# Other places in SBUF for g and its halves, and another tile for the first chunk's lower attended values

## The chip, the cores and the metric

The kernel runs on one core of a Trainium2 chip. What counts is the device time in microseconds of one execution, the median over several runs. Beside it there is one execution taken by the hardware profiler: its page gives totals for each engine, the chain of waits that ended last, and groups of instructions; its trace can be asked for single instructions and for stretches of time. TensorE is written PE there (PEld is its loading of stationary tiles, which overlaps the matmuls), VectorE is DVE, ScalarE is ACT, GpSimd is POOL, SyncE is SP, which issues all the transfers here. L488 means line 488 of the kernel before.

## What is computed

An attention layer is followed by a feed-forward layer. Cut to what matters:

```python
# q, k, v: (4, 8, 768, 64) = batch, heads, positions, head dim
k_sum = k.reshape(B, H, nb, 32, D).max(axis=3)      # 24 block maxima
v_sum = v.reshape(B, H, nb, 32, D).mean(axis=3)     # 24 block means
scores_l = scale * q @ k.T, kept where |i - j| < 16, else -1e9
scores_s = scale * q @ k_sum.T + log(32)
a = softmax(concat([scores_l, scores_s]))
x = a @ concat([v, v_sum])                          # -> (3072, 512)

h = x @ w_in                                        # (3072, 2048)
r = maximum(h, 0)
g = s * (r * r) + b
out = g @ w_out                                     # (3072, 512)
```

All is float32. The attention part is small; the two products of the feed-forward layer are most of the work.

## The kernel before

**Chunks and blocks.** The 3,072 positions are cut into 12 chunks (c = 0 to 11) of T = 256. In a chunk the attention is done for four pairs of heads, and its result, the attended values, stands as 128 partitions by 4 blocks of 256 columns. The feed-forward layer goes through 16 blocks of 128 hidden units (f = 0 to 15). For each f the hidden product (function `hidden`, line 444) makes a PSUM tile `ph` of 128 x 256 out of the attended values and the weights w_in of the block; `activate` makes r, the square of its positive part; `scaled` makes g = s r + b on GpSimd (line 466); and the projection (`project`, line 488) adds the block's part to two PSUM tiles `po` of 128 x 512, one for each half of the chunk's positions. `evict` copies them out and stores them.

**Products in three terms.** From chunk 1 on, and for the second half of the blocks in chunk 0 (the list THREE), each float32 operand is split into an upper part rounded to the matmul's shorter type (fp32r) and a lower part that holds the rest: weights into wh and wl, attended values into xh and xl, g into gh and gl. A product is then three matmul terms: lower times upper, upper times lower, upper times upper. In the hidden product the stationary operand is a block of weights and the moving operand is xh or xl, 256 columns wide. In the projection it is the other way round: gl or gh is stationary, and wh or wl, 512 columns wide, moves. The splits are made by `attended` and `attended_low` (line 410) for x and by `split_rows` (lines 471 and 473) for g. The first half of the blocks in chunk 0 is computed in plain float32, with an undivided g0 that uses the buffers of gh.

**The first chunk's halves.** Chunk 0's attended values stand in float32. `first_upper` and `first_lower` (line 419) make their halves x0h and x0l, which the hidden products of chunk 0's blocks 8 to 15 read.

**Where tiles lie.** Tiles come from pools; a pool gives each tag a fixed number of buffers, and a new tile of the tag takes a buffer once all readers of the tile before it are done. The ones that matter:

| pool | tags | what for |
|---|---|---|
| slots | slot, 16 buffers of 4 KB | raw weights as they are loaded, the pairs of wh, at the start also kq, vn, pT0, x0h, x0l |
| wring | ring, 33 of 2 KB | whole weights wf, lower weights wl |
| stage | stage, 4 of 3 KB | raw k and v, results on their way out |
| p2 | xh 2, xl 2 of 4 KB; r 2, g 2, gh 8, gl 7 of 1 KB; pT, pr and small ones | the attended values, r, g and its halves |
| p3 | qk 4, vw 4 | the attention's operands |

In the compiled program the pools lie one behind the other in SBUF, p3 behind p2 at the end.

**What sets the order.** Each engine runs its instructions in the order in which the program writes them. For the first part, up to somewhat over a fifth of the span, that is a list written out by hand (FIRST_ORDER): `Xh` and `Xl` are the two halves of chunk 0, `y1.0` the lower attended values of chunk 1's first pair, `y2.0` those of chunk 2, `iN` and `oN` the loads of weights, `H`, `J`, `G`, `g` and `P` the hidden product, activation, scaling, split and projection. After that a regular plan takes over: four hidden products, then the projection of four blocks whose g has been made meanwhile, with the attention of the next chunk set between them. In the trace a full visit is thus 48 hidden matmuls (4 blocks x 3 terms x 4 slices), then 24 projection matmuls (4 blocks x 2 halves x 3 terms). SP issues the transfers in order too, and holds the next ones back while one waits for its buffer.

Of the kernel before, what the change touches and what calls it, by code (L numbers as in the profile page):

```python
# [11 lines left out]
F32 = mybir.dt.float32  # L12
F32R = mybir.dt.float32r
# [6 lines left out]
P = 128  # L20
# [9 lines left out]
T = NSUB * SUB  # L30
# [4 lines left out]
NKC = DM // P  # L35
# [9 lines left out]
def windowed_attention_then_relu2_ffn(ctx, tc, qk, vwin, kt, vt, kq, vrow, wp, out):  # L45
# [5 lines left out]
    slots = ctx.enter_context(tc.tile_pool(name="slots", bufs=NF))  # L51
    wring = ctx.enter_context(tc.tile_pool(name="wring", bufs=2 * NF + 1))
    stage = ctx.enter_context(tc.tile_pool(name="stage", bufs=4))
    p2 = ctx.enter_context(tc.tile_pool(name="p2", bufs=2))
    p3 = ctx.enter_context(tc.tile_pool(name="p3", bufs=3))
    ps_po = ctx.enter_context(tc.tile_pool(name="ps_po", bufs=2, space=bass.MemoryType.PSUM))
    ps_h = ctx.enter_context(tc.tile_pool(name="ps_h", bufs=2, space=bass.MemoryType.PSUM))
# [1 line left out]
    ps_t = ctx.enter_context(tc.tile_pool(name="ps_t", bufs=1, space=bass.MemoryType.PSUM))  # L59
    ps_v = ctx.enter_context(tc.tile_pool(name="ps_v", bufs=1, space=bass.MemoryType.PSUM))  # L60

    ident = const.tile([P, P], F32, name="ident")
    sb_col = const.tile([P, 2], F32, name="sb_col")
    s_col, b_col = sb_col[:, 0:1], sb_col[:, 1:2]
# [177 lines left out]
    qk_t, vw_t, ps_of, pr_of, mn_of, sm_of, pt_of, pT_of, o_of, xt, xl = ({} for _ in range(11))  # L242
# [153 lines left out]
    def attended_part(c, p):  # L396
        kcs = slice(p, p + (1 if c < 2 else 2))
        return kcs, o_of[c, p][:, : (kcs.stop - p) * T].rearrange("p (k t) -> p k t", t=T)
# [6 lines left out]

    def attended_low(c, p):
        if p == 0:
            xl[c] = p2.tile([P, NKC, T], F32R, name="xl")
        kcs, o = attended_part(c, p)
        nc.vector.tensor_tensor(xl[c][:, kcs], o, xt[c][:, kcs].bitcast(F32), ALU.subtract)  # L410

# [3 lines left out]
        copy(other, xt["first"], xt[0])  # L415

    def first_lower():
        xl["first"] = slots.tile([P, NKC, T], F32R, name="x0l", tag="slot")
        nc.vector.tensor_tensor(xl["first"], xt[0], xt["first"].bitcast(F32), ALU.subtract)


# [37 lines left out]

    def scaled(c, f, other=False):  # L460
        if c == 0 and f not in THREE:
            g = p2.tile([P, T], F32, name="g0", tag="gh", bufs=8)
        else:
            g = p2.tile([P, T], F32, name="g")
        gg[c, f] = (g,)
        (nc.vector if other else nc.gpsimd).tensor_scalar(g, r_of.pop((c, f)), s_col, b_col, ALU.mult, ALU.add)  # L466

    def split_rows(c, f):
        (g,) = gg[c, f]
        gh = p2.tile([P, T], F32R, name="gh", tag="gh", bufs=8)  # L470
        nc.vector.tensor_copy(gh, g)  # L471
        gl = p2.tile([P, T], F32R, name="gl", bufs=7)
        nc.vector.tensor_tensor(gl, g, gh.bitcast(F32), ALU.subtract)  # L473
        gg[c, f] = gh, gl

# [60 lines left out]
    def of(fn, s):  # L536
# [5 lines left out]
        "W": keep_warm, "K": k_max, "k": fill_k, "Z": scores_of_maxima, "S": scores, "M": masked, "E": exps,  # L542
        "N": normalize, "T": transposes, "C": turned, "V": values, "U": values_of_means, "R": mean_of_rows,
        "L": load_k, "F": mean_done, "t": fill_v, "X": attended, "y": attended_low, "Xh": first_upper, "Xl": first_lower,
        "Ai": of(scale_weights, "in"), "Ao": of(scale_weights, "out"), "Bi": of(convert_weights, "in"),
        "Bo": of(convert_weights, "out"), "D": lambda f: convert_weights(("in", f), ("out", f)),
        "Y": hidden_part, "H": hidden, "J": activate, "G": scaled, "g": split_rows, "P": project, "O": evict,
        "hi": of(upper_weights, "in"), "ho": of(upper_weights, "out"), "li": of(lower_weights, "in"),
        "lo": of(lower_weights, "out"),
# [22 lines left out]
    for c in range(2, NC):  # L572
        bi, ci = place(c)
        for p in range(NPAIR):
            base, v_at = NF * (c - 1) - 1, (9, 10, 4, 5)[p]
            tr = 8 + 4 * (p // 2)
            lags = (1, 1, 1, 2, (12, 13, 11, 11)[p], tr, tr, 16, 17)
            m, e0, e1, n, fv, tr, tu, va, xa = (base + lag for lag in lags)
            if ci == 0:
                then(base - 12 + p, LOAD, load_k, bi, p)  # L580
                then(base - 7 + p, ATT, k_max, bi, p)
                if p < 2:
                    for third in range(3):
                        then(base + v_at - 5 + third, LOAD, load_v, bi, p, third)
                        then(base + v_at - 1 + third // 2, ATT, v_sum, bi, p, third)
                    then(base + v_at + 1, ATT, v_mean, bi, p)
            then(base - 6, LOAD, load_unit, c, p)
            then(base + v_at, LOAD, load_values, c, p)
            then(base - 2, ATT, fill_k, c, p)
            for j in range(2):  # L590
                then(base, VISIT, scores, c, p, j)
                then(m, NEXT if p < 2 else ATT, masked, c, p, j)
                then((e0, e1)[j], NEXT if p < 2 else ATT, exps, c, p, j)
            then(n, ATT, normalize, c, p)
            then(fv, ATT, fill_v, c, p)
            then(tr, PE_ATT, transposes, c, p)
            then(tu, CHAIN, turned, c, p)
            then(va, VISIT, values, c, p)
            if p % 2 == 0:
                then(xa, ATT, attended, c, p)  # L600
                then(xa, ATT, attended_low, c, p)
# [4 lines left out]
    for i in range(NF, NC * NF):  # L606
        c, j = divmod(i, NF)
        f = steps(c)[j]

        then(i - i % 4, HID, hidden, c, f)  # L610
        for stage_of in (activate, scaled, split_rows):
            then(i, CHAIN, stage_of, c, f)
        then((i + 4) | 3, PROJ, project, c, f)
        if j == NF - 1:
            for t in range(T // P):
                then((i + 4) | 3, EVICT, evict, c, t)
# [60 lines left out]
```

## Time and profile before

| | |
|---|---|
| median of 3 runs | 631.02 us (630.45 to 631.4) |
| the profiled execution | 630.93 us, its span 629.2 us |
| granted TensorE clock | 1.00 |
| busy: PE, PEld | 616.5 us (98%), 550.7 us (88%) |
| busy: DVE, ACT, POOL | 328.3 us (52%), 308.7 us (49%), 187.7 us (30%) |
| transfers | 66.45 MB, most of them in the first fifth |

How to read it: the records of matmuls are pipelined and overlap, so a record's length is not its cost. Its cost is the distance from its start to the start of the next one. In the chain of waits such records are merged, so "5.50 PE po L488 x24" says that 24 projection matmuls in a row took 5.50 us of the chain. A row of a cut into stretches gives the stretch, its length, and then the busy time and the number of instructions of each engine in it.

### The profile page before, as it was taken

To read this page: it belongs to the slowest core of one execution; us is meant where nothing else is said; L and a number is where in the kernel's file an instruction comes from. 1 tells how busy PE (TensorE), PEld (TensorE's weight loads), DVE (VectorE), ACT (ScalarE), POOL (GpSimd) and SP (SyncE) were. 2 spreads that over 40 slices of the span, in tenths; PEclk is the share of its full clock that TensorE was granted. 3 is DMA by queue.
4 is the path that set the end of the run, shared out by engine and by line. 5 is a ranking of instruction groups with operands and counts; after the bars stand their busy time and mean duration, and the time that the engine had idled before them with its cause. 6 is when DMAs were issued, how large, how long until landed. Compare 5 with 4: busy or idle time off the path is not lost.

```text
span 629.2 us, 14328 instructions
## 1 busy us (share of the span) xinstructions
PE 616.5 (98%) x5330; PEld 550.7 (88%) x5330; DVE 328.3 (52%) x1092; ACT 308.7 (49%) x939; POOL 187.7 (30%) x351
## 2 busy tenths in 40 slices
PE   6999999999999999999999999999999999999997
PEld 5757878989989998999899999998998999899896
DVE  6999899865354246345454335336435324523311
ACT  4999975453463364265245426436345336323321
POOL 3126442211511422322242331341151151232211
PEclk9999999999999999999999999999999999999999
DMA  8999503006205015203502211600710500200000
GB/s 333 413 416 416 222 26 126 17 2 190 79 18 181 1 44 200 74 19 102 165 20 87 94 44 38 236 19 1 218 62 7 181 0 19 85 2 1 34 1 33
DMA packets 26997, 66.45 MB, mean 106 GB/s; under 512 B 3824, under 2 KB 3824, under 8 KB 26928
## 3 DMA queue, kind: packets, MB, share of 16 engines
q1 hardware_dynamic: 26928, 65.54, 29.3%
q8 instruction: 42, 0.69, 0.5%
q14 instruction: 27, 0.22, 0.1%
HBM read 59.09 MB, written 6.29 MB: 104 GB/s over the span
## 4 chain that ended last, share of the span: by engine, by line
PE 87%; DVE 4%; ACT 2%; issue 1%; POOL 1%; DVEq 0%; POOLq 0%; ACTq 0%
PE po L488 40%; PE ph L444 38%; PE pav L394 3%; PE pt L358 3%; PE ps L308 3%; DVE wf_out L141 1%; POOL g L466 1%; DVE wl_in L155 1%; DVE wf_in L141 0%; DVE wf_in L139 0%; ACT r L458 0%; DVE wf_out L139 0%; ACT wraw L125 0%; ACT wraw L126 0%; ACT r L452 0%
## 5 line engine op out<-in xcount | busy, mean ns | idle before, releaser
L466 POOL TENSOR_SCALAR g<-r,sb_col 128x256 f32<-128x256 f32 x189 | 127.1, 673 | 379.2 <-ACT r L458 256.0
L471 DVE CAST gh<-g 128x256 fp32r<-128x256 f32 x184 | 54.9, 298 | 244.0 <-POOL g L466 244.0
L452 ACT ACTIVATE r<-ph 128x256 f32<-128x256 f32 x179 | 67.6, 378 | 206.1 <-PE ph L444 187.0
L488 PE MATMUL po<-wh,gl 128*128 128x512 f32 x368 | 146.3, 397 | 0.0
L488 PE MATMUL po<-wh,gh 128*128 128x512 f32 x368 | 145.0, 394 | 0.0
L488 PE MATMUL po<-wl_out,gh 128*128 128x512 f32 x368 | 144.2, 392 | 0.0
L444 PE MATMUL ph<-xh,wl_in 128*128 128x256 f32 x704 | 109.9, 278 | 0.1
L444 PE MATMUL ph<-xl,wh 128*128 128x256 f32 x704 | 108.8, 276 | 0.0
L444 PE MATMUL ph<-xh,wh 128*128 128x256 f32 x704 | 108.7, 276 | 0.0
L473 DVE TENSOR_TENSOR gl<-g,gh 128x256 fp32r<-128x256 f32 x184 | 85.8, 466 | 33.6 <-PE po L488 16.4
L444 PEld LDWEIGHTS ph<-xh,wl_in 128*128 128x128 f32 x704 | 96.8, 188 | 4.8 <-issue 0.5
L444 PEld LDWEIGHTS ph<-xl,wh 128*128 128x128 f32 x704 | 93.6, 188 | 0.0
L444 PEld LDWEIGHTS ph<-xh,wh 128*128 128x128 f32 x704 | 93.0, 188 | 0.0
L339 ACT ACTIVATE pr<-pr,mn 128x120 f32<-128x120 f32 x176 | 67.0, 382 | 38.6 <-DVE mn L326 38.4
L458 ACT ACTIVATE r<-r 128x256 f32<-128x256 f32 x184 | 77.0, 418 | 15.2 <-DVE r L454 9.7
L488 PEld LDWEIGHTS po<-wh,gl 128*128 128x128 f32 x368 | 69.1, 188 | 14.8 <-issue 1.4
L488 PEld LDWEIGHTS po<-wh,gh 128*128 128x128 f32 x368 | 69.2, 188 | 14.3
L488 PEld LDWEIGHTS po<-wl_out,gh 128*128 128x128 f32 x368 | 69.2, 188 | 13.8
L270 POOL COPY vw<-vsum 24x256 f32<-24x256 f32 x88 | 41.7, 503 | 20.9 <-DMA vsum<-vmean 9.5
L230 ACT COPY o<-po 128x512 f32<-128x512 f32 x24 | 14.0, 589 | 42.3 <-PE po L488 41.3
L339 ACT ACTIVATION_READ_ACCUMULATOR pr<-pr,mn 128x1 f32 x176 | 33.0, 187 | 0.0
L349 DVE TENSOR_TENSOR pr<-pr,rs 128x480 f32<-128x480 f32 x48 | 32.0, 666 | 1.7
(90 smaller groups left out, 565.4 us busy)
## 6 DMA issues: line engine op xcount, KB each, us to landing
wraw<-in_wp_dram SPq DMA_DIRECT2D x32, 512.0 KB
qk<-in_qk_dram SPq DMA_DIRECT2D x44, 369.0 KB
vw<-in_vwin_dram SPq DMA_DIRECT2D x48, 256.0 KB
out_dram<-o SPq DMA_DIRECT2D x24, 256.0 KB
kraw<-in_kt_dram SPq DMA_DIRECT2D x12, 384.0 KB
vraw<-in_vt_dram SPq DMA_DIRECT2D x12, 252.0 KB
kq<-in_kq_dram SPq DMA_DIRECT2D x4, 512.0 KB
vraw<-in_vt_dram SPq DMA_DIRECT2D x6, 264.0 KB
```

The source lines that it names most:

```text
L270: nc.gpsimd.tensor_copy(vw_t[c, p][WIN:KR, e], vsum[bi][WIN : WIN + NB, 2 * p + e, :].unsqueeze(1).to_broadcast([NB, NSUB, D]),)
L308: nc.tensor.matmul(o, qi, kw[r, i, :], start=True, stop=True)
L339: nc.scalar.activation(pr, pr, AF.Exp, bias=mn_of[c, p][:, n : n + 1], scale=-1.0, accum_out=sm_of[c, p][:, n : n + 1])
L349: nc.vector.tensor_tensor(pr, pr, rs.unsqueeze(2).to_broadcast([P, 4, KR]), ALU.mult)
L358: nc.tensor.transpose(pt_of[c, p][:KR, n * P : (n + 1) * P], pr[:, n, :], ident)
L444: nc.tensor.matmul(ph, w[:, kc * P : (kc + 1) * P], x[:, kc], start=(n == 0), stop=(n == len(terms) - 1))
L452: nc.scalar.activation(r, ph, AF.Relu)
L458: nc.scalar.activation(r, r, AF.Square)
L466: (nc.vector if other else nc.gpsimd).tensor_scalar(g, r_of.pop((c, f)), s_col, b_col, ALU.mult, ALU.add)
L471: nc.vector.tensor_copy(gh, g)
L473: nc.vector.tensor_tensor(gl, g, gh.bitcast(F32), ALU.subtract)
L488: nc.tensor.matmul(po[t], a[:, t * P : (t + 1) * P], w, start=(f == steps(c)[0] and n == 0), stop=(f == steps(c)[-1] and n == len(terms) - 1),
```

## The change

Three things are done. A new pool `pg` is opened between p2 and p3; its first tile, `gap`, is 128 bytes a partition and is never used. The tiles g, g0, gh and gl come out of `pg`, with the same numbers of buffers as before. And x0l, the lower half of chunk 0's attended values, is a tile of p2's tag xl, whose two buffers the later chunks' xl use too, and no longer a tile of the slots.

```diff
+    pg = ctx.enter_context(tc.tile_pool(name="pg", bufs=1))
     p3 = ctx.enter_context(tc.tile_pool(name="p3", bufs=3))
...
+    pg.tile([P, 32], F32, name="gap")
...
     def attended_low(c, p):
         if p == 0:
-            xl[c] = p2.tile([P, NKC, T], F32R, name="xl")
+            xl[c] = p2.tile([P, NKC, T], F32R, name="xl", tag="xl")
...
     def first_lower():
-        xl["first"] = slots.tile([P, NKC, T], F32R, name="x0l", tag="slot")
+        xl["first"] = p2.tile([P, NKC, T], F32R, name="x0l", tag="xl")
...
     def scaled(c, f, other=False):
         if c == 0 and f not in THREE:
-            g = p2.tile([P, T], F32, name="g0", tag="gh", bufs=8)
-        else:
-            g = p2.tile([P, T], F32, name="g")
+            g = pg.tile([P, T], F32, name="g0", tag="gh", bufs=8)
+        else:
+            g = pg.tile([P, T], F32, name="g", bufs=2)
...
     def split_rows(c, f):
         (g,) = gg[c, f]
-        gh = p2.tile([P, T], F32R, name="gh", tag="gh", bufs=8)
+        gh = pg.tile([P, T], F32R, name="gh", tag="gh", bufs=8)
         nc.vector.tensor_copy(gh, g)
-        gl = p2.tile([P, T], F32R, name="gl", bufs=7)
+        gl = pg.tile([P, T], F32R, name="gl", bufs=7)
         nc.vector.tensor_tensor(gl, g, gh.bitcast(F32), ALU.subtract)
```

No instruction is added or taken away, and the written order stays.

## The prediction

> **What bounds the kernel now.** I read the engine totals of the page first, then the chain of waits in order of time, then the totals cut at two points of that chain, and last the timeline of TensorE's records.
>
> ```profile
> span 629.2 us, 14328 instructions
> PE 616.5 (98%) x5330; PEld 550.7 (88%) x5330; DVE 328.3 (52%) x1092; ACT 308.7 (49%) x939; POOL 187.7 (30%) x351
> ...
> PE 87%; DVE 4%; ACT 2%; issue 1%; POOL 1%; DVEq 0%; POOLq 0%; ACTq 0%
> ```
>
> The chain that ends last is TensorE for 87% of the span. Its pieces show where that begins:
>
> ```profile
> 81.13 0.61 DVE wl_in L155
> 81.88 3.11 PE ph L444 x24
> ...
> 120.15 2.74 PE ph L444 x24
> 122.90 2.02 PE pav L394 x64
> 124.92 1.80 PE ps L308 x64
> 126.72 4.33 PE po L488 x18
> ...
> 136.70 5.60 PE po L488 x24
> 142.30 5.46 PE ph L444 x48
> ...
> 253.43 5.46 PE ph L444 x48
> ...
> 259.76 5.50 PE po L488 x24
> ```
>
> Up to 81.88 us the chain goes through VectorE and ScalarE, and from there through TensorE alone. The same span cut at those points:
>
> ```profile
> core 0: us, PE busy (x) PEld busy (x) DVE busy (x) ACT busy (x) POOL busy (x), PEclk, DMA share, GB/s
> 0.00:81.88 81.88, 72.81 (x754) 56.56 (x755) 72.44 (x208) 70.73 (x181) 31.46 (x60) 1.00 0.87 346
> 81.88:126.72 44.84, 44.74 (x423) 40.12 (x423) 41.60 (x120) 23.55 (x70) 15.47 (x27) 1.00 0.19 59
> 126.72:629.20 502.48, 498.90 (x4155) 454.05 (x4154) 214.24 (x766) 214.41 (x690) 140.74 (x264) 1.00 0.22 71
> ```
>
> From 81.88 to 126.72 us VectorE is busy for 41.60 of 44.84 us, so a faster TensorE would soon wait for it. After 126.72 us VectorE and ScalarE are each busy for 214 of 502 us: there TensorE's pace alone sets the end, at a granted clock of 1.00. The same cut for the projection's line alone counts its matmuls in that last stretch:
>
> ```profile
> 126.72:629.20 502.48, 238.89 (x1002) 185.10 (x1002) 1.00 0.22 71
> ```
>
> So a nanosecond on each projection matmul is worth 1.0 us. Their pace is 5.50/24 = 229 ns; that of the hidden matmuls, half as wide, 5.46/48 = 114 ns. Neither count changes, nor any instruction: the change can act only through placement and through the order in which buffers come free.
>
> **The change, part by part.** *Where things come to lie.* From the allocations of the compiled program before: slots and ring tiles (the weights) start 768 bytes past a multiple of 2,048, xh and xl 1,984 past one, g, gh and gl 960 past a multiple of 1,024. Taking 17 tiles of 1 KB out of p2 brings its end to byte 191,424; the gap tile takes 128, the ring of gh starts at 191,552, g at 199,744, gl at 201,792, all 64 past a multiple of 1,024, that is 128 bytes on modulo 1,024. xl moves down by 8,192, unchanged by that measure. p3 moves up by 128.
>
> *The engines that write g, gh and gl.* 189 for g and 184 for gh, with as many for gl behind them:
>
> ```profile
> L466 POOL TENSOR_SCALAR g<-r,sb_col 128x256 f32<-128x256 f32 x189 | 127.1, 673 | 379.2 <-ACT r L458 256.0
> L471 DVE CAST gh<-g 128x256 fp32r<-128x256 f32 x184 | 54.9, 298 | 244.0 <-POOL g L466 244.0
> ```
>
> The rings keep 2, 8 and 7 buffers, and the buffers of g and gl alternate between two offsets already. I cost them at nothing. The cover is the idle time: 244.0 us of VectorE's before gh. Gone, it would show as idle time before po.
>
> *The weight loads of the projection.* This is the one place where 128 bytes could matter, since gl and gh are loaded into TensorE 1,002 times on the path. The trace does hold a difference by placement. First the hidden matmuls on x0h and x0l, which lie in slots, then those on xh and xl, which lie in p2:
>
> ```profile
> 82.43 0.64 PE L444 MATMUL ph<-x0l,wh 128*128 128x256 f32 x4
> 82.91 0.64 PE L444 MATMUL ph<-x0h,wh 128*128 128x256 f32 x4
> ...
> 240.95 0.39 PE L488 MATMUL po<-wl_out,gh 128*128 128x512 f32 x1
> 241.18 0.39 PE L488 MATMUL po<-wh,gh 128*128 128x512 f32 x1
> 241.41 0.64 PE L444 MATMUL ph<-xh,wl_in 128*128 128x256 f32 x4
> 241.88 0.62 PE L444 MATMUL ph<-xl,wh 128*128 128x256 f32 x4
> 242.34 0.62 PE L444 MATMUL ph<-xh,wh 128*128 128x256 f32 x4
> 242.79 0.62 PE L444 MATMUL ph<-xh,wl_in 128*128 128x256 f32 x4
> ```
>
> Start to start, four take 0.48 us on x0 and 0.455 on xh and xl: 120 against 114 ns, the same instruction. Two readings fit: the stationary tile's offset, its start less the moving one's modulo 512 (weights at 256, xh and xl at 448: 0 under x0, 320 under xh; gh at 448, later 64, against weights at 256: 192 now, 320 after the change), or something about the moving operand alone. In the first the edit gives the projection the offset of the faster hidden matmuls; in the second it does nothing, as gh and gl are never moving operands. The matmuls at the seams tell them apart to a degree. While the last projection matmul of a visit streams, TensorE loads not a gl but the first wl_in, at offset 0:
>
> ```profile
> 241.18 0.65 PEld L444 LDWEIGHTS ph<-xh,wl_in 128*128 128x128 f32 x4
> ```
>
> That matmul takes 241.41 - 241.18 = 0.23 us, as its neighbours do. The other way round, while a last hidden matmul streams, gl is loaded, at offset 0:
>
> ```profile
> 235.46 0.62 PE L444 MATMUL ph<-xh,wh 128*128 128x256 f32 x4
> 235.91 0.39 PE L488 MATMUL po<-wh,gl 128*128 128x512 f32 x1
> ```
>
> That group takes 0.45 us, none of the 120 ns of x0. So changing the stationary tile's offset changes nothing I can see; the moving operand decides. Bounds from rows: down by 6 ns a matmul (the 120 - 114 of x0), up by 4 ns ((5.60 - 5.50)/24, the slower of two cadences that the projection shows). I take 0, by the seams, which are nearest, and keep -6.0 and +4.2 us for the range. One thing stays open: offset 320 under a projection matmul is never seen.
>
> [...]
>
> *x0l in the xl ring.* The one VectorE instruction and its readers stay:
>
> ```profile
> L419 DVE TENSOR_TENSOR x0l<-xh,x0h 128x1024 fp32r<-128x1024 f32 x1 | 1.2, 1218 | 0.0
> L444 PE MATMUL ph<-x0l,wh 128*128 128x256 f32 x32 | 5.1, 282 | 0.0
> ```
>
> x0l now lies like xl. Of its 32 matmuls 8 fall into the piece of 3.11 us at 81.88 us; at 6 ns each that is -0.05 us, and I take it, since here the moving operand moves. Its bounds are -0.05 and +0.05. The ring has two buffers: chunk 1's xl takes one, x0l the other, and chunk 2's must wait for chunk 1's last hidden matmuls or for x0l's, which end with the piece at 81.88 us. Chunk 1's end at 120.15 + 2.74 = 122.89 us, and chunk 2's xl is written at
>
> ```profile
> 125.87 0.68 DVE L410 TENSOR_TENSOR xl<-pav,xh 128x512 fp32r<-128x512 f32 x1
> ```
>
> because it needs the pav that ends at 124.92. The new wait is over 3 us earlier: cost 0. If that cover were gone, gh and gl behind it on VectorE would be late, and with them the projection at 126.72.
>
> *A slot less taken.* From x0l's writing on, one slot more is free for weight loads, so loads that SP holds back for a slot can issue earlier, and with them the qk, vw and kraw loads queued behind. The transfers gain nothing while the DMA engines are full, and they are until the last ones:
>
> ```profile
> 60.00:70.00 10.00, 9.72 (x84) 7.97 (x77) 9.96 (x23) 9.43 (x19) 3.02 (x3) 1.00 1.03 396
> 70.00:80.00 10.00, 10.00 (x72) 8.97 (x71) 8.08 (x19) 9.00 (x20) 5.35 (x7) 1.00 0.18 71
> ```
>
> ScalarE, which takes the weights first, waited for a load only once:
>
> ```profile
> L125 ACT ACTIVATE wraw<-wraw 128x512 f32<-128x512 f32 x32 | 21.9, 685 | 7.3 <-DMA wraw<-in_wp_dram 7.3
> ```
>
> So 0, with ±0.5 us for a stage in which VectorE and ScalarE are busy for 9 to 10 of 10 us and small shifts change who goes first.
>
> *Sum.* The profiled execution took 630.93 us, its span of 629.2 and 1.7 around it; the median of the runs is 631.02. 630.93 + 0 - 0.05 + 0 + 0 = **630.9 us**.
>
> **The rivals.** *A, the projection takes the hidden matmuls' offset and pace.* For it: x0 against xh, and that the offset becomes the one of xh exactly. Against it: the two seams. Price: by the projection's own two cadences 4.2 ns, by x0's difference 6 ns, so 4.2 to 6.0 us over 1,002 matmuls: 624.9 to 626.7 us; a weak form, pace exactly twice the hidden one (2 x 114 = 228), 1.3 us: 629.6.
>
> *B, the projection falls into its slower cadence.* One visit, at 136.70, takes 5.60 us where all its like take 5.50, with the same tiles in the same places: two cadences exist, and a start differing by little picks one. If the new offset makes the slower one usual, 1002/24 = 42 visits x 0.10 = 4.2 us: 635.1. It decides from the point where about 13 of 42 visits are slow. Against it: before, all but one go fast.
>
> *C, the change doesn't do what it says ahead of 126.72 us:* the ring hands chunk 2 a buffer late, or a stalled load delays a conversion. Price 0.5 to 3 us, the cover above: up to 634. Against it: the order of events quoted.
>
> **How the numbers follow.** Within 0.2% (±1.26 us) is about what a measurement of this kernel can't tell from no change. My forecast has 0.47, own range 629.9 to 631.9; A 0.34, B 0.14, C 0.05. Of the forecast's 0.47, 0.02 falls out on each side; of A, 0.02 is the weak form that stays within. Faster 0.34, same 0.45, slower 0.21. The range takes in A's full price and the forecast, and C and the near part of B: 624.7 to 634.0 us.
>
> **What would show it.** Right: visits of 24 projection matmuls at 5.50 us and of 48 hidden at 5.46 to 5.47, TensorE alone on the chain from about 82 us, x0l's four in 0.46 us. A: visits at 5.30 to 5.40. B: at 5.60. C: an idle VectorE ahead of xl near 125.87, or ScalarE waiting on wraw past 20 us. A pace of the projection that differs by over 1.3 ns makes the prediction wrong.

## The result, and the profile after

The changed kernel takes 637.56 us (median of 4 runs, 637.21 to 637.73), the kernel before 631.05 us on the same chip (4 runs, 630.45 to 631.4): a ratio of 1.0103 with an interval of 1.0086 to 1.0121. It is slower by 6.5 us, above the predicted range.

The page of the changed kernel, engine totals and the chain's shares:

```profile
span 635.5 us, 14328 instructions
PE 623.3 (98%) x5330; PEld 553.5 (87%) x5330; DVE 328.7 (52%) x1092; ACT 308.5 (49%) x939; POOL 183.7 (29%) x351
...
PE 88%; DVE 4%; ACT 4%; issue 1%; DMA 1%; POOL 1%; SPq 0%; DVEq 0%; POOLq 0%; ACTq 0%
```

The instructions are as many as before. TensorE's matmuls are busier by 6.8 us and its weight loads by 2.8; VectorE and ScalarE differ by 0.4 and 0.2 us, GpSimd is less busy. The span is 6.3 us longer. The span of the changed kernel, cut at the same two events of its chain as in the prediction (the first piece of TensorE alone, and the 18 projection matmuls behind chunk 2's scores):

```profile
core 0: us, PE busy (x) PEld busy (x) DVE busy (x) ACT busy (x) POOL busy (x), PEclk, DMA share, GB/s
0.00:81.75 81.75, 73.21 (x755) 57.30 (x755) 72.44 (x208) 70.73 (x181) 29.83 (x60) 1.00 0.87 346
81.75:126.66 44.91, 44.82 (x423) 39.97 (x423) 41.60 (x120) 23.49 (x69) 14.86 (x27) 1.00 0.19 59
126.66:635.50 508.84, 505.25 (x4155) 456.17 (x4154) 214.66 (x766) 214.30 (x690) 139.03 (x265) 1.00 0.21 70
```

Against before the first stretch is 0.13 us shorter, the second 0.07 longer, and the last 508.84 - 502.48 = 6.36 longer. So all the time is lost where TensorE's pace alone sets the end, at the same granted clock of 1.00, with VectorE and ScalarE as idle as before. Which of its matmuls lost it is told by the same cut for one tile alone: the hidden product's `ph` in the kernel before (first the stretch and its length, then TensorE's busy time with the count; the row for `po` before, 238.89, stands in the prediction),

```profile
126.72:660.00 533.28, 225.39 (x1920) 224.75 (x1920) 0.00 (x0) 60.43 (x160) 1.00 0.20 67
```

and `po`, then `ph`, in the changed kernel:

```profile
126.72:660.00 533.28, 242.85 (x1002) 184.92 (x1002) 12.94 (x22) 1.00 0.20 67
126.72:660.00 533.28, 227.71 (x1920) 226.94 (x1920) 0.00 (x0) 60.40 (x160) 1.00 0.20 67
```

The projection lost 242.85 - 238.89 = 3.96 us, the hidden product 227.71 - 225.39 = 2.32 us. The sum, 6.28, is the growth of the span. I call these two numbers the po sum and the ph sum below: with 238.89 and 225.39 before, their changes add up to the change of the span in every run, to within 0.6 us.

The chain of the changed kernel over the length of one chunk shows both parts (start, length, engine, tile, line, matmuls; in this and the later chains the short pieces of the attention between the visits are left out):

```profile
225.81 5.79 PE po L490 x24
231.61 5.46 PE ph L446 x48
237.07 5.59 PE po L490 x24
242.66 5.65 PE ph L446 x48
249.19 5.61 PE po L490 x24
254.80 5.46 PE ph L446 x48
261.13 5.61 PE po L490 x24
266.74 5.45 PE ph L446 x48
```

Of the 39 full projection visits in the last stretch, the 9 right behind the attention's scores take 5.79 or 5.80 us where they took 5.70 to 5.72. The other 30 take 5.59 to 5.61 where all but one took 5.49 to 5.51. So **all** of them are slower, not one. And of the four hidden visits shown, whose tiles the gap didn't move, one takes 5.65 instead of 5.46. Over the whole trace 15 of the 40 full hidden visits are of the long kind, against 1 of 40 before, and always the same three in every eight (eight visits are two chunks): a fixed pattern, no noise. Nothing stands between 5.46 and 5.65: hidden visits have two cadences, 5.46/48 = 114 and 5.65/48 = 118 ns a matmul, and each visit keeps one of them (by the starts in the trace, both halves of a visit run at the same pace to 0.2 ns). Two records of projection matmuls, seven apart, give their pace without the edges:

```profile
237.37 0.40 PE L490 MATMUL po<-wh,gh 128*128 128x512 f32 x1
...
239.00 0.39 PE L490 MATMUL po<-wh,gl 128*128 128x512 f32 x1
```

(239.00 - 237.37)/7 = 233 ns, against 229 before.

### The profile page after: what moved, and what is told of

Same layout as the page of the kernel before. It is cut to its first block, busy times and chain, and to the rows that moved or that the text cites. A ratio compares the mean times of both kernels' runs of the same rounds, so it can differ in the third digit from the quotient of the medians.

```text
span 635.5 us, 14328 instructions
## 1 busy us (share of the span) xinstructions
PE 623.3 (98%) x5330; PEld 553.5 (87%) x5330; DVE 328.7 (52%) x1092; ACT 308.5 (49%) x939; POOL 183.7 (29%) x351
## 4 chain that ended last, share of the span: by engine, by line
PE 88%; DVE 4%; ACT 4%; issue 1%; DMA 1%; POOL 1%; SPq 0%; DVEq 0%; POOLq 0%; ACTq 0%
PE po L490 41%; PE ph L446 38%; PE pav L396 3%; PE pt L360 3%; PE ps L310 3%; DMA wraw<-in_wp_dram 1%; ACT pr L341 1%; DVE wf_out L143 1%; POOL g L468 1%; ACT wraw L128 1%; ACT r L460 1%; DVE wf_in L143 1%; ACT wraw L127 1%; ACT wh L232 0%; ACT r L454 0%
## 5 line engine op out<-in xcount | busy, mean ns | idle before, releaser
L473 DVE CAST gh<-g 128x256 fp32r<-128x256 f32 x184 | 54.6, 297 | 249.3 <-POOL g L468 249.3
L490 PE MATMUL po<-wh,gl 128*128 128x512 f32 x368 | 148.1, 402 | 0.0
L272 POOL COPY vw<-vsum 24x256 f32<-24x256 f32 x88 | 40.1, 484 | 20.2 <-DMA vsum<-vmean 9.0
```

The source lines that it names most:

```text
L272: nc.gpsimd.tensor_copy(vw_t[c, p][WIN:KR, e], vsum[bi][WIN : WIN + NB, 2 * p + e, :].unsqueeze(1).to_broadcast([NB, NSUB, D]),)
L490: nc.tensor.matmul(po[t], a[:, t * P : (t + 1) * P], w, start=(f == steps(c)[0] and n == 0), stop=(f == steps(c)[-1] and n == len(terms) - 1),
```

## The experiments

All edits are against the changed kernel, and all but the moved tiles stays. Two numbers describe a kernel: the start of the stationary tile less the start of the moving tile, modulo 256 bytes (that 256 is the period is a result of the runs), once for the projection (gh or gl against the weights), once for the hidden product (weights against xh or xl). I write them **g** and **x**. The kernel before has g 192 and x 64, the changed one g 64 and x 64. Each run's ratio is to the kernel before on the same chip, 630.75 to 631.12 us.

### Which part of the change it is

e1 takes the gap away and leaves the rest of the change:

```diff
-    pg.tile([P, 32], F32, name="gap")
```

> The changed kernel without the gap tile: g, gh and gl stay in their own pool behind xl, but start 960 past a multiple of 1,024 again, as before the change; x0l stays in the xl ring. Theory 'offset' (the 128 bytes alone slow the projection, from 229 to 233 ns a matmul): visits of 24 projection matmuls at 5.50 us, hidden visits all at 5.46, time 630.5 to 631.5. Theory 'region' (another pool order, g some KB away from where it was): visits stay at 5.60, time 637. Theory 'ring' (x0l in the xl ring and one slot tile less shift the start of the steady part): the time stays at 636 to 637.5 too.

e2 puts x0l back among the slots and leaves the gap:

```diff
-        xl["first"] = p2.tile([P, NKC, T], F32R, name="x0l", tag="xl")
+        xl["first"] = slots.tile([P, NKC, T], F32R, name="x0l", tag="slot")
```

> The changed kernel with x0l back in a slot; the pool of g with its 128 bytes of gap stays. Theories 'offset' and 'region': 637 to 638, visits of the projection at 5.60. Theory 'ring': 631, visits at 5.50.

e5 puts the 128 bytes ahead of everything. g, gh and gl then lie at the bytes where the changed kernel has them, but weights, xh and xl have moved along:

```diff
-    pg.tile([P, 32], F32, name="gap")
+    const.tile([P, 32], F32, name="pad")
```

> No gap tile, but a tile of 128 bytes ahead of everything in the first pool, so that weights, attended values, g and its halves all lie 128 bytes further on. gh and gl stand at the very bytes where they stand in the changed kernel; against the weights they stand as before the change (offset 192). Theory 'relative' (what counts is the stationary tile's start against the moving one's): 630.5 to 631.5, visits of the projection at 5.50. Theory 'absolute' (what counts is where gh and gl lie by themselves): 637, visits at 5.60.

e4 makes the gap 320 bytes, so that g is 0:

```diff
-    pg.tile([P, 32], F32, name="gap")
+    pg.tile([P, 80], F32, name="gap")
```

> The changed kernel with a gap of 320 bytes instead of 128: gh and gl start 256 past a multiple of 1,024, so their offset against the weights is 0, the one that the hidden matmuls on x0h have (120 ns for 256 columns where xh takes 114). Theory 'relative', with x0 as its example: slower than the changed kernel, 4 ns or more on each of 1,002 matmuls beyond 233, 640 or more. Theory 'moving operand alone', which the prediction held: no change against a gap of 0, 631. Should the offset act otherwise than in x0, the visits of the projection come out between 5.30 and 5.60 us.

| run | g, x | us | ratio to before | po sum | ph sum | long hidden visits |
|---|---|---|---|---|---|---|
| before | 192, 64 | 631.05 | | 238.89 | 225.39 | 1 of 40 |
| changed | 64, 64 | 637.56 | 1.0103 [1.0086, 1.0121] | 242.85 | 227.71 | 15 |
| e1, no gap | 192, 64 | 630.93 | 0.9999 [0.9990, 1.0008] | 238.73 | 225.39 | 1 |
| e2, x0l in slots | 64, 64 | 637.44 | 1.0104 [1.0089, 1.0119] | 242.98 | 227.71 | 15 |
| e5, all moved by 128 | 192, 64 | 630.66 | 0.9996 [0.9987, 1.0006] | 238.68 | 225.20 | 0 |
| e4, gap 320 | 0, 64 | 636.29 | 1.0086 [1.0071, 1.0101] | 237.38 | 232.66 | 40 |

The gap is the whole loss, and x0l's move has no part in it that these runs can tell. The chain of e1, with the visits of before back:

```profile
235.92 5.49 PE po L489 x24
241.41 5.47 PE ph L445 x48
247.75 5.51 PE po L489 x24
253.27 5.46 PE ph L445 x48
```

e5 tells where tiles lie from how they lie to each other: g and its halves are at the same bytes as in the slow kernel, and the time is that of before, 630.66 us. Its chain:

```profile
235.68 5.49 PE po L490 x24
241.17 5.47 PE ph L446 x48
247.51 5.51 PE po L490 x24
```

So it is the **relation** of the two tiles of a matmul. e4 then split the loss in two in a way that I had not reckoned with. The projection becomes faster than it has ever been, and every hidden visit becomes long, with none of its tiles moved. The chain of e4:

```profile
231.60 5.65 PE ph L446 x48
237.25 5.44 PE po L490 x24
242.69 5.66 PE ph L446 x48
249.22 5.49 PE po L490 x24
```

and its two sums, `po` and `ph`:

```profile
126.72:660.00 533.28, 237.38 (x1002) 185.03 (x1002) 12.94 (x22) 1.00 0.20 67
126.72:660.00 533.28, 232.66 (x1920) 231.81 (x1920) 0.00 (x0) 60.47 (x160) 1.00 0.20 67
```

-1.51 on the one and +7.27 on the other: 5.8 us, as much as its span grew.

### What the period is, and what the hidden product's own offset does

e6 has a gap of 64 bytes, e7 of 256; with a period of 512 they would be new offsets, with one of 256 e6 repeats e4 and e7 the kernel before:

```diff
-    pg.tile([P, 32], F32, name="gap")
+    pg.tile([P, 16], F32, name="gap")
```

> A gap of 64 bytes: offset of gh and gl against the weights 256 (so far 192 gave 229 ns a projection matmul, 320 gave 233, 0 gave 227). Theory 'period 256' (offsets 0 and 256 are alike): as with a gap of 320, visits of the projection at 5.44 to 5.49 us, all hidden visits at 5.65, 636. Theory 'period 512, changing evenly with the offset': between 192 and 320, so 231 ns, 5.55 us, 634. The theory of the prediction, that the stationary tile's place doesn't matter, has fallen and expects 631.

```diff
-    pg.tile([P, 32], F32, name="gap")
+    pg.tile([P, 64], F32, name="gap")
```

> A gap of 256 bytes: offset 448. Theory 'period 256': as with no gap (offset 192), visits at 5.50 and hidden visits at 5.46, 631. Theory 'period 512': between the cases of 320 and 0, with hidden visits partly or all at 5.65, so 636.

e8 and e9 keep g at 0 and move xh and xl by a pad in p2, of 128 bytes in e8 and of 64 in e9 (gap 256):

```diff
-    pg.tile([P, 32], F32, name="gap")
+    pg.tile([P, 48], F32, name="gap")
+    p2.tile([P, 32], F32, name="pad", bufs=1)
```

> A tile of 128 bytes ahead of p2 and a gap of 192: gh and gl at offset 0 against the weights as with the gap of 320 (projection at 227 ns), while xh and xl lie 128 bytes on, so that the weights' offset against them is 192 instead of 320. Theory 'hand-over' (the hidden visits were slow with the gap of 320 because a projection at offset 0 leaves TensorE in the slower cadence, whatever xh's place): hidden visits at 5.65 again, 636. Theory 'own offset' (each kind of matmul has its cadences by its own offset): hidden visits change, to 5.46 if 192 serves them as it serves the projection, and then the time is 40 x 0.19 = 7 us less, 629.

```diff
-    pg.tile([P, 32], F32, name="gap")
+    pg.tile([P, 64], F32, name="gap")
+    p2.tile([P, 16], F32, name="pad", bufs=1)
```

> As the run before, with 64 bytes ahead of p2 and a gap of 256: projection at offset 0, hidden matmuls at offset 256. Theory 'hand-over': hidden visits at 5.65, 636. Theory 'own offset': whatever 256 gives the hidden matmuls; with period 256 that is the offset of x0h, 120 ns each, 5.75 a visit, 640.

| run | g, x | us | ratio to before | po sum | ph sum | long hidden visits |
|---|---|---|---|---|---|---|
| e6, gap 64 | 0, 64 | 636.53 | 1.0095 [1.0078, 1.0112] | 236.57, two records missing | 232.68 | 40 |
| e7, gap 256 | 192, 64 | 630.41 | 0.9993 [0.9984, 1.0002] | 238.50 | 225.24 | 0 |
| e8, pad 128 | 0, 192 | 637.23 | 1.0103 [1.0088, 1.0118] | 237.61 | 232.71 | 40 |
| e9, pad 64 | 0, 0 | 641.40 | 1.0168 [1.0153, 1.0183] | 237.72 | 236.62 | 40, longer still |

e6 is e4 and e7 is the kernel before, in both sums: the pattern repeats after 256 bytes, not after the 512 of the prediction. The projection's sum stays at 237.4 to 237.7 for g 0, whatever x is. The hidden product has an offset scale of its own: at x 0 its visits take yet longer. From the chain of e9:

```profile
232.97 5.75 PE ph L447 x48
238.72 5.47 PE po L491 x24
244.19 5.75 PE ph L447 x48
```

### The rest of the square

e10 has a gap of 192 bytes (g 128):

```diff
-    pg.tile([P, 32], F32, name="gap")
+    pg.tile([P, 48], F32, name="gap")
```

> A gap of 192 bytes, the last of the four offsets modulo 256: 128 for the projection (192 gave 229 ns, 64 gave 233, 0 gave 227). Theory 'evenly': between 64 and 192, 231 ns and 5.55 us a visit. Theory 'hand-over' (the hidden visits, whose own offset stays 64, take the cadence in which the projection leaves them): after a projection slower than at 192, mixed or all at 5.65, so 634 to 638. Theory 'four separate cases': anything; a projection at 224 ns or less with hidden visits at 5.46 would give 626.

e11 keeps the gap of 128 and pads p2 by 192; e12 has the same pad and no gap; e13 has the gap and pads p2 by 128:

```diff
     pg.tile([P, 32], F32, name="gap")
+    p2.tile([P, 48], F32, name="pad", bufs=1)
```

> 192 bytes ahead of p2 and a gap of 128: projection at offset 0 (227 ns), hidden matmuls at offset 128, the last one not yet tried there (64 gave 113 or 118 ns, 192 gave 118, 0 gave 120). Theory 'hand-over': a projection at offset 0 leaves the hidden matmuls slow whatever their own offset, 5.65 or more a visit, 636. Theory 'own offset': if 128 is the opposite of 0 it is the free one for them, 113 ns, 5.45 a visit, and the whole 628.5 to 629.

```diff
-    pg.tile([P, 32], F32, name="gap")
+    p2.tile([P, 48], F32, name="pad", bufs=1)
```

> 192 bytes ahead of p2 and no gap: both the projection and the hidden matmuls at offset 128. Theory 'own offset': the projection as in the run with a gap of 192, the hidden visits as in the run before this. Theory 'hand-over': hidden visits as the projection leaves them.

```diff
     pg.tile([P, 32], F32, name="gap")
+    p2.tile([P, 32], F32, name="pad", bufs=1)
```

> 128 bytes ahead of p2 and a gap of 128: projection at offset 192 as before the change (229 ns), hidden matmuls at offset 192 instead of 64. Theory 'hand-over': a projection at 192 leaves the hidden matmuls fast, 5.46, so 631. Theory 'own offset' (with projection at 0 and hidden at 192 the hidden visits took 5.65): 5.65 again, 638.

| run | g, x | us | ratio to before | po sum | ph sum | long hidden visits |
|---|---|---|---|---|---|---|
| e10 | 128, 64 | 635.45 | 1.0070 [1.0055, 1.0085] | 242.11 | 226.59 | 10 of 40 |
| e11 | 0, 128 | 641.73 | 1.0169 [1.0152, 1.0186] | 237.99 | 236.70 | 40: 39 as in e9, one of 5.69 |
| e12 | 128, 128 | 645.00 | 1.0220 [1.0205, 1.0235] | 242.17 | 235.57 | 40: 21 as in e9, 19 of 5.69 or 5.70 |
| e13 | 192, 192 | 638.51 | 1.0118 [1.0103, 1.0134] | 239.09 | 232.58 | 40 |

The two sums follow their own offset each: the projection's 242.1 to 242.2 at g 128, 238.0 at g 0, 239.1 at g 192; the hidden product's 235.6 to 236.7 at x 128 and 232.6 at x 192. e12, bad in both, is the slowest kernel of all, 13.9 us behind before, and its two sums give (242.17 - 238.89) + (235.57 - 225.39) = 13.5:

```profile
126.72:660.00 533.28, 242.17 (x1002) 185.49 (x1002) 12.94 (x22) 1.00 0.20 67
126.72:660.00 533.28, 235.57 (x1920) 234.62 (x1920) 0.00 (x0) 60.44 (x160) 1.00 0.20 67
```

e13 is the test between the two theories: its projection runs at the old offset and pace, and still all hidden visits are long, so a hidden visit has a cadence by its own offset and not only by the projection ahead. The hope of e11, that x 128 would be the free offset, failed: 5.76 a visit where 5.45 was expected. Only at x 64 do hidden visits take 5.46, and there only some of them.

### One half of g at a time

If each matmul paid for its own offset alone, a kernel with gl at one offset and gh at another would have a projection pace in between, one part of gl's and two of gh's (gh is stationary in two of the three terms). e14 moves gl alone by 128 bytes, e16 by 64, with a pool of its own behind pg:

```diff
-    pg.tile([P, 32], F32, name="gap")
+    pgl.tile([P, 32], F32, name="gap")
...
-        gl = pg.tile([P, T], F32R, name="gl", bufs=7)
+        gl = pgl.tile([P, T], F32R, name="gl", bufs=7)
```

> Only gl lies 128 bytes further on (a gap tile ahead of gl alone): offset 64 for gl, 192 as before the change for gh. Theory 'each load by itself' (a matmul's pace goes with the tile that is loaded while it streams; gl under one term of three): a third of the change's 4.6 ns on the projection, 230.3 ns, 5.53 a visit. Theory 'gh sets the hidden cadence' (the gh of the last matmuls ahead of a hidden visit): hidden visits stay at 5.46, time 632.5. Theory 'the whole pace sets it': some hidden visits at 5.65, 633 to 635.

(e16 has the same with `[P, 16]`.)

> Only gl lies 64 bytes further on: offset 0 modulo 256 for gl, 192 for gh. Theory 'each load by itself': the term under which gl is loaded goes from 232 to 227 ns, the mean from 228.8 to 227.2, 5.46 a visit. Theory 'gh sets the hidden cadence': hidden visits stay at 5.46, so 1,002 x 1.6 ns less than before, 629.3: faster than both kernels. Theory 'the whole pace sets it': hidden visits at 5.65 as with both at 0, 636.

e15 moves gh (and g) alone by 128 bytes, e17 by 64: gl stands in a pool ahead of the gap.

```diff
     pg.tile([P, 32], F32, name="gap")
...
-        gl = pg.tile([P, T], F32R, name="gl", bufs=7)
+        gl = pgl.tile([P, T], F32R, name="gl", bufs=7)
```

> Only gh (and g) lie 128 bytes further on, gl as before the change. Theory 'each load by itself': two thirds of the change's 4.6 ns, 231.9 ns, 5.56 a visit. Theory 'gh sets the hidden cadence': hidden visits mixed 5.46 and 5.65 as in the changed kernel, 636. Theory 'the whole pace sets it': 634 to 636, fewer slow visits than in the changed kernel.

(e17 has the same with `[P, 16]` for the gap.)

> Only gh (and g) lie 64 bytes further on: offset 0 for gh, 192 for gl. Theory 'each load by itself': the terms under which gh is loaded go to 227 ns, that under gl stays at 232, mean 228.3. Theory 'gh sets the hidden cadence': hidden visits all at 5.65, 638. Theory 'the whole pace sets it': hidden visits at 5.46 or mixed, 631 to 635.

| run | g of gl, of gh | us | ratio to before | po sum | ph sum | long hidden visits |
|---|---|---|---|---|---|---|
| e14 | 64, 192 | 634.94 | 1.0060 [1.0043, 1.0077] | 242.39 | 225.79 | 5 of 40 |
| e15 | 192, 64 | 634.79 | 1.0060 [1.0045, 1.0075] | 241.32 | 226.74 | 10 |
| e16 | 0, 192 | 634.76 | 1.0062 [1.0047, 1.0077] | 239.97 | 228.19 | 16 |
| e17 | 192, 0 | 633.77 | 1.0043 [1.0028, 1.0058] | 240.80 | 226.31 | 8 |

By distances between starts (from the 4th to the 18th of each of the 39 full visits, averaged), the paces are 232.9, 232.0, 230.2 and 231.0 ns. By shares of the paces with both halves alike (228.9 at g 192, 233.3 at 64, 227.8 at 0) they should be 230.4, 231.8, 228.5 and 228.2. Only e15 fits. So that simple account falls: one moved term of three costs e14 nearly all of the 4 us (242.39 against 238.89), and mixing a good offset (0) with a fair one (192) is worse than either alone. From the chain of e16, whose two pure relatives have 5.44 and 5.49 in this place:

```profile
236.63 5.54 PE po L491 x24
242.17 5.66 PE ph L447 x48
```

A second idea fell too, that gh (the tile loaded last before a hidden visit) picks the hidden cadence: e16, with gh unmoved, has 16 long visits, e17, with gh moved, 8.

### Finer steps

e18 has a gap of 32 bytes, e19 of 224:

```diff
-    pg.tile([P, 32], F32, name="gap")
+    pg.tile([P, 8], F32, name="gap")
```

> A gap of 32 bytes: offset 224, halfway between 192 (229 ns, hidden visits at 5.46) and 0 (227 ns, hidden visits at 5.65). Theory 'steps of 64 bytes': as one of the two, so 631 or 636. Theory 'finer than 64': its own pace; the case that would beat both kernels is a projection at 227 with hidden visits at 5.46, 629.

```diff
-    pg.tile([P, 32], F32, name="gap")
+    pg.tile([P, 56], F32, name="gap")
```

> A gap of 224 bytes: offset 160, halfway between 128 (232 ns, a quarter of the hidden visits slow, 635.5) and 192 (229 ns, 631). Theory 'steps of 64 bytes': as one of the two. Theory 'finer than 64': its own pace, from 226 to 236 ns, 629 to 638.

| run | g, x | us | ratio to before | po sum | ph sum | long hidden visits |
|---|---|---|---|---|---|---|
| e18, gap 32 | 224, 64 | 640.51 | 1.0163 [1.0149, 1.0177] | 242.79 | 230.88 | 31 of 40 |
| e19, gap 224 | 160, 64 | 634.52 | 1.0065 [1.0053, 1.0078] | 242.84 | 224.87 | 0 |

Thirty-two bytes are enough. g 224 lies between 192 and 0, the two best, and its projection is as slow as at 64. These two runs are the cleanest view of the two hidden cadences. They have the same tiles for the hidden product, the same pace of the projection and the same po sum within 0.05 us, and differ by 6.0 us, which is the ph sum: 31 long visits in the one, none in the other. The chain of e18,

```profile
226.56 5.80 PE po L490 x24
232.36 5.45 PE ph L446 x48
237.81 5.60 PE po L490 x24
243.41 5.66 PE ph L446 x48
```

and of e19:

```profile
231.44 5.45 PE ph L446 x48
236.89 5.60 PE po L490 x24
242.48 5.47 PE ph L446 x48
```

So it is not the projection's pace that picks the cadence: it is 233 ns in e18, in e19 and in the changed kernel, with 31, 0 and 15 long visits. The place in the plan counts too. In e18 the nine short visits are those behind a full projection visit that follows the scores (5.80 above). In e15 the visits in that place are long, as is the first of the stretch, and all others are short:

```profile
225.07 5.77 PE po L491 x24
230.84 5.65 PE ph L447 x48
236.50 5.57 PE po L491 x24
242.06 5.45 PE ph L447 x48
```

No run beats the kernel before: e7 has the lowest median, 630.41 us, and its interval holds 1. The pair that would, a projection at g 0 (-1.5 us) followed by short hidden visits, didn't come about in any run: at g 0 all 40 were long.

## Why the prediction was wrong

**What bounds the kernel: right.** The loss is TensorE's pace after 126.66 us to within 0.1 us, and the rate of 1 us for 1 ns on each projection matmul held: visits longer by 0.09 to 0.10 us are 4 ns a matmul, and the po sum grew by 3.96 us.

**Where things come to lie: right in bytes, wrong in the measure.** I compared tiles modulo 512. e6 and e7 show 256: e6 takes 636.53 us where e4 takes 636.29, e7 0.9993 of the time before.

**The engines that write g, gh and gl: right.** The same two groups after, as long as before and as idle (VectorE waits 249.3 us ahead of gh, where it waited 244.0):

```profile
L468 POOL TENSOR_SCALAR g<-r,sb_col 128x256 f32<-128x256 f32 x189 | 125.9, 666 | 390.8 <-ACT r L460 260.3 <-issue 32.8 <-DVE gh L473 31.9
L473 DVE CAST gh<-g 128x256 fp32r<-128x256 f32 x184 | 54.6, 297 | 249.3 <-POOL g L468 249.3
```

**The weight loads of the projection: the step that failed.** It ended in "the moving operand decides ... I take 0, by the seams". Neither moving tile was touched by the gap, and the projection lost 4 us. Of the two readings the first, the offset of the two tiles, was the true one, as e1 and e5 show, but not with the gain that it was given: the offset of the faster hidden matmuls made the projection slower. Three things went wrong in this step.

- The seams were read as if they stood for whole visits. Averaged over the trace of the kernel before (the one slow projection visit and the one long hidden visit left out), they do show nothing, as was said: the last projection matmul ahead of a hidden visit takes 231.5 ns and the same term inside the visits 231.4, the last hidden matmul ahead of a projection visit 113.3 and those inside 113.5. But whole visits at the offset of these seams run at another pace: 228 ns at g 0 (e4) and 120 ns at x 0 (e9). So a seam doesn't tell what a visit at its offset does. Why not is open; e14 to e17, where a mix of offsets isn't the sum of its parts, point the same way.
- "Offset 320 under a projection matmul is never seen" was the honest sentence of that step, and it should have kept the forecast from 0. The lower bound came from the hidden product, on the thought that what is fast there is fast here. It isn't: x 64 gives the hidden product its shortest visits, g 64 the projection one of its longest, and g 0 is best for the projection where x 0 is among the worst for the hidden product.
- Nothing was set down for the hidden product, since its tiles stay. It lost 2.32 us.

So the place of the two operands was not free in this kernel: 128 bytes between them cost 6.5 us of 631, and the offsets of e12 cost 13.9.

**x0l and the slot: right.** x0l's four matmuls take 82.75 - 82.28 = 0.47 us (0.48 before, 0.46 forecast), and chunk 2's xl is written at the same 125.87 us:

```profile
82.28 0.63 PE L446 MATMUL ph<-x0l,wh 128*128 128x256 f32 x4
82.75 0.63 PE L446 MATMUL ph<-x0h,wh 128*128 128x256 f32 x4
...
125.87 0.68 DVE L412 TENSOR_TENSOR xl<-pav,xh 128x512 fp32r<-128x512 f32 x1
```

The ring made nobody wait, and TensorE's own part of the chain starts at 81.75 us instead of 81.88, inside the 0.5 us allowed for the slot. e2 confirms it: with x0l back, 637.44 us. One reading was a little off: the cover was called over 3 us, and 125.87 - 122.89 is 2.98.

**The sum.** 630.93 + 3.96 + 2.32 = 637.21 us, the time of the profiled execution after.

**The rivals.** A, a faster projection, had the sign wrong. C did not happen. B is what happened, as far as it went: its price was 42 visits x 0.10 = 4.2 us, and the po sum grew by 3.96. I had given it 0.14 because "before, all but one go fast"; but the old offset's cadences said nothing of the new offset's: 1 of 39 full visits was slow before and all 39 after, those that don't follow the scores at 5.59 to 5.61 us, the length of that one visit of 5.60. B's 635.1 was left outside the range, although the step on the weight loads had kept its +4.2 us for it. And 2.3 us more than B came from the hidden visits, for which a row was at hand as well. Before, too, one hidden visit of 40 was long, and it stands right ahead of the projection visit of 5.60 at 136.70:

```profile
131.05 5.66 PE ph L444 x48
```

e1 has both of these visits, e5 and e7 have neither. Which of the two brings about the other, no run shows.

## What to carry to other kernels

Where TensorE alone sets the end, a new allocation in SBUF can be a change to the matmuls, as the 128 bytes were here (6.5 us): compare for each kind of matmul the start of the stationary tile with that of the moving one, before and after, here modulo 256 bytes, and where that number changes, reckon with a change (here up to 2.2% slower, and no kernel faster than before) and measure it, rather than reading it off another kind of matmul or off one at a seam. Look at the visits of the chain one by one: a kind whose visits come in two lengths, here 5.46 and 5.65, has a second cadence, which a change elsewhere may make usual (here 1 long visit of 40 before, 15 after, 40 in e4). And judge a placement by the whole loop, since in e4 the matmuls whose tiles were moved gained 1.5 us and the others lost 7.3.

## What the runs showed of the hardware

- **In these runs a matmul's pace went with where its two operands lay to each other.** By distances between starts inside visits, with both halves of g alike, a projection matmul took 228 ns at g 0 (in e4 the visits that don't follow the scores run from 5.44 to 5.50 us), 229 at 192, 232 to 233 at 128, and 233 at 64, 160 and 224. A hidden matmul took 113.3 to 113.5 or 117.8 ns at x 64, 117.8 at 192, 120 at 0, and 118.6 to 120 at 128. A shift by 256 bytes gave the same time at the two offsets where it was tried (e6 636.53 us against 636.29 in e4, e7 630.41 us, 0.9993 of the time before), a shift of all these tiles together by 128 bytes changed nothing that the runs can tell (e5, 630.66 us, 0.9996 of the time before), and 32 bytes against the kernel before cost 9.8 us (e18, 640.51 against 630.75 on its chip). The shortest projection visits took 5.44/24 = 227 ns a matmul (e4).
- **The same matmuls on the same tiles had two cadences.** At x 64 a hidden visit took 5.46 or 5.65 us as a whole. Which of them went with where g and its halves lay (0 long visits of 40 for g 160, at most 1 for 192, then 10, 15, 31 and 40 for 128, 64, 224 and 0, while the hidden product's own tiles stay) and with the visit's place in the plan (behind a full projection visit that follows the scores 5.65 us in e15 and 5.45 in e18, behind the next one 5.45 and 5.66).

Four things stay open. What in the chip has a period of 256 bytes, no run shows. What picks a hidden visit's cadence isn't known either. That the projection ahead hands it on is argued: VectorE and GpSimd write g and its halves meanwhile (in the changed kernel a g is begun at 235.88 us, a gh at 236.47 and a gl at 236.87, in the hidden visit that runs from 231.61 to 237.07), at places that move with the gap, and no run separates the two. Against these writers speaks that a long visit is long evenly, in both halves. The pattern of the changed kernel repeats every two chunks, which is as often as the two buffers of xh and xl come round, but in e10, e15 and e18 it repeats every chunk, with the same two buffers. The gap also moves p3, the attention's operands, which no run moved alone; e16 and e17 move it by the same 64 bytes as e6, with other sums, so its place alone doesn't set them. And whether g 0 can go with short hidden visits was not settled.
